# A written engine order for the late stage of an attention-and-feed-forward kernel, and earlier reloads of two chunks' partial outputs

## The chip, the cores and the metric

One core of one Trainium2 chip runs the kernel. The metric is the device time of one execution in microseconds (us), lower is better. The engines that matter are TensorE (PE in the profile; its weight loads are PEld), VectorE (DVE), ScalarE (ACT), GpSimd (POOL) and SyncE (SP), which here only issues DMAs.

## What is computed

```
scores = q @ k^T / 8, masked: heads 0 to 3 see 32 keys back, heads 4 to 7 every 4th of 128
attn   = softmax(scores);  x = (attn @ v), heads side by side: 4608 tokens x 512
h      = x @ w_in                                   # 512 x 2048
g      = max(h, 0) + log1p(exp(-abs(h)))
out    = g @ w_out                                  # 2048 x 512
```

All in float32. A float32 factor goes to TensorE as a high and a low part in the type fp32r (the cast is ACT's, the subtraction DVE's), and three products (high x high, high x low, low x high) make one.

## The kernel before

The 4608 tokens are nine chunks of 512, and the 2048 columns of `w_in` are sixteen tiles of 128 (`ff`). Chunks 0 and 1 are worked while the weights arrive and are decoded: 32 slots of one chunk and one `ff`, in the runs `RUNS`; a slot is twelve 512-column products for h (`h_part`) and, two slots later, twelve for out (`o_part`). Chunk 0 stops after six `ff` and chunk 1 has its first ten; their partial sums go to DRAM (`kept`), and when the runs resume and end, the partial sum is loaded into a buffer `ob` (`ob_tile`) and DVE adds it to what PSUM holds.

Chunks 2 to 8 make the **late stage**, a loop over 56 pairs of `ff` tiles (eight per chunk). A pair makes its h by seven block products instead of eight. Each of the seven steps of `steps` is six 256-column matmuls into one of two PSUM banks (`h_x`, `h_y`), one DVE instruction that brings the bank out (`aside`, to `temps` or `hs`), and then one group of three 512-column matmuls for an output of an earlier tile (`outputs`; two groups in the seventh step). A product overwrites or adds to its bank, so it waits for DVE to have read what the same bank held. After steps 6 and 7 the tile's softplus follows: three activations on ACT, an add on DVE (`e`), the cast `gh` on ACT and the subtraction `gl` on DVE.

Between them stands the attention of the next chunk, in four groups of two heads: scores on PE (`s_ps`), mask and maximum on DVE (`s`, `nm`), eight exponentials on ACT, the sum's reciprocal on DVE (`sm`, `ri`), the division on POOL, a transpose on DVE (`squares`), its way through DRAM by DMA (`turned`, `pt`), and values on PE (`a_ps`), which ACT copies to `x_full`. From `x_full` DVE forms four `sums` (`combine`) and seven blocks are split in high and low (`split`) for the next chunk's products. `convert` brings the weights to the form that the seven products want, six pairs of them during the slots and two in the late stage.

What sets the order: the program's text gives one order, in which `attend`, `combine`, `split` and `convert` are placed by a list of events with due times in slots (`at`, `pump`). The recording layer's scheduler then orders each engine by its own estimate, except instructions that are pinned with `tc.keep_in_program_order`: all matmuls, the DMAs of `load_dma`, and, while `opening` is set (the first seven slots), everything that goes through `pin`. So in the late stage DVE and ACT stand as the scheduler put them.

```
def pin(ins):
    if opening:
        tc.keep_in_program_order(ins)
```

The last output group of a chunk frees its PSUM bank by a copy to `ob` (ACT or DVE, L865 and L867) and goes out from there.

Of the kernel before, what the change touches and what calls it, by code (L numbers as in the profile page):

```python
# [90 lines left out]
def tile_windowed_attention_softplus_ffn(  # L91
# [32 lines left out]
    opening = True  # L124

    def pin(ins):

        if opening:
            tc.keep_in_program_order(ins)
# [114 lines left out]
    def combine(c, n):  # L244

        if n % 2 == 0:
            combined[c, n // 2] = const.tile([P, 2, 2, HALF], F32, name="sums", tag=f"x_{'cd'[n // 2]}")
        dst = [combined[c, j // 2][:, j % 2] for j in range(n + 1)]
# [6 lines left out]
        nc.vector.tensor_tensor(out=dst[n], in0=a, in1=b, op=op)  # L255
# [4 lines left out]
    def split(c, name):  # L260
        if name not in blocks:
# [3 lines left out]
        dst, n = blocks[name], int(name[1:])  # L265
        if name[0] == "a":
            src = x_block(c, n // 10 - 1, n % 10 - 1)
        else:
            src = combined[c, (n - 1) // 2][:, (n - 1) % 2]
        nc.scalar.copy(out=dst[:, 0], in_=src)  # L270
        nc.vector.tensor_tensor(out=dst[:, 1], in0=src, in1=dst[:, 0].bitcast(F32), op=ALU.subtract)

    class Group:
# [50 lines left out]
        def maximum(self):  # L324
# [15 lines left out]
            for r in range(2):  # L340
# [6 lines left out]
                nc.vector.scalar_tensor_tensor(  # L347
                    out=dst, in0=src, scalar=1.0 / 8.0, in1=m, op0=ALU.mult, op1=ALU.add
                )
            nc.vector.tensor_reduce(out=nm, in_=self.blocks, axis=AX.X, op=ALU.max, negate=True)  # L350
# [53 lines left out]
        def turn_squares(self):  # L404

            squares = const.tile([P, WKEYS // SQ, NB, SQ], F32, name="squares", tag="q1")
            nc.vector.transpose(out=squares, in_=self.blocks.rearrange("p t (b k) -> p b t k", k=SQ))
# [97 lines left out]
    events = []  # L505

    def at(when, part, *what):
        events.append((when, len(events), part, what))
# [12 lines left out]
    def pump(now):  # L521
        while events and events[0][0] <= now:
            _, _, part, what = events.pop(0)
            part(*what)

# [56 lines left out]
    def ob_tile(m, resumed, c):  # L582
        if resumed and c:
            if m % 2 == 0:
                obs["both"] = const.tile([P, 2, CH], F32, name="ob", tag=f"x_{'cd'[m // 2]}")
            obs[m] = obs["both"][:, m % 2]
        else:
            obs[m] = dpool.tile([P, CH], F32, name="ob", tag="a")
        if resumed:
            nc.sync.dma_start(out=obs[m], in_=kept[c, m])  # L590

    def o_part(i, m):
# [6 lines left out]
        if m == 0:  # L599
# [3 lines left out]
            if final:  # L603
# [8 lines left out]
        if final:  # L612
# [11 lines left out]
            if m == 0:  # L624
                ob_tile(3, resumed, c)

# [49 lines left out]
    opening = False  # L676
# [10 lines left out]
    def weight_sum(p, j):  # L687
# [8 lines left out]
        nc.vector.tensor_tensor(  # L696
            out=sums[p, j].rearrange("p k n -> p (k n)"), in0=parts[:, 0], in1=parts[:, 1], op=ALU.add
        )

    def weight_13(p):  # L700
# [3 lines left out]
        nc.vector.tensor_tensor(out=d[:, 0], in0=two[:, 0], in1=one[:, 0], op=ALU.subtract)  # L704
        nc.vector.tensor_tensor(out=d[:, 1], in0=two[:, 1], in1=two[:, 0], op=ALU.subtract)

    def weight_24(p):
        d, one, two = diffs[p], sums[p, 0], sums[p, 1]
        nc.vector.tensor_tensor(out=two[:, 1], in0=two[:, 1], in1=d[:, 0], op=ALU.subtract)
        nc.vector.tensor_tensor(out=one[:, 1], in0=one[:, 1], in1=two[:, 1], op=ALU.subtract)  # L710

    def parted(high, low, src):
        nc.scalar.copy(out=high, in_=src)
        nc.vector.tensor_tensor(out=low, in0=src, in1=high.bitcast(F32), op=ALU.subtract)
# [17 lines left out]
    def convert(p):  # L732
# [5 lines left out]
        weight_split_24(p)  # L738

# [37 lines left out]
    for j in range(NPR):  # L777
        attend(FIRST, j, 10.8 + 3.5 * j, (0.5, 2.8, 3.2, 4.5))
# [4 lines left out]
    for p in range(NPAIR):  # L783
        at(20.5 + 1.9 * p if p < EARLY else 36.5 + 3 * (p - EARLY), convert, p)
    for c in range(FIRST + 1, NCH):
        base = 2 * NFF + (c - 1 - FIRST) * NFF
        for j in range(NPR):
            attend(c, j, base + (3.73 * j - 2.1 if c == FIRST + 1 else 3.5 * j - 1.5), (0.5, 2.25, 2.65, 4.5))
        for n in range(4):
            at(base + 13.7 + 0.1 * n, combine, c, n)  # L790
# [254 lines left out]
```

## Time and profile before

| | |
|---|---|
| three runs | 907.26, 908.34, 908.34 us; median 908.34 |
| the profiled execution | 907.07 us, its span 905.3 us |
| granted TensorE clock, mean | 0.998 |
| late stage, first product of pair 0 to first of pair 55 | 236.50 to 882.25 us |

The profile is of one execution. The span runs from the first to the last instruction; about 1.8 us of the execution's time lie around it. PE's busy time counts a pipelined matmul as longer than the step to the next, so PE at 97% says little; how long a pair takes from first product to first product says more.

### The profile page before, as it was taken

What the parts mean: (1) busy time and instruction counts of PE and PEld (TensorE: products, weight loads), DVE (VectorE), ACT (ScalarE), POOL (GpSimd) and SP (SyncE); (2) the same over time, 40 slices, a digit from 0 to 9 for tenths busy, and PEclk for the clock granted to TensorE, in tenths of its full rate; (3) what the DMA queues carried; (4) which work ended last, traced back from release to release, by engine and by line L of the source; (5) the groups of instructions that cost most, each with busy time, mean ns of one, the idle gap of its engine ahead of it and who ended that gap; (6) DMA issues with size and microseconds to landing.
All of it is one profiled execution on the core that took longest, in us unless ns stands there. A gap on an engine that the chain in (4) does not pass through costs nothing.

```text
span 905.3 us, 18339 instructions
## 1 busy us (share of the span) xinstructions
PE 879.8 (97%) x6972; PEld 742.3 (82%) x6978; DVE 634.9 (70%) x1242; ACT 542.0 (60%) x1348; POOL 64.1 (7%) x46
## 2 busy tenths in 40 slices
PE   6899999999999999999999999999999999999998
PEld 3567888788788888888888888888888888889987
DVE  4799998997696586657666675668665866575444
ACT  6677677775555576556555665556555655564443
POOL 1320000000000000000000001000000000000000
PEclk9999999999999999999999999999999999999999
DMA  9989334333555546554555446545654455424223
GB/s 295 315 277 375 131 135 155 129 104 107 190 171 162 163 141 217 170 162 156 198 183 180 161 159 203 185 147 171 203 166 157 166 200 164 152 94 158 98 94 117
DMA packets 79095, 156.41 MB, mean 173 GB/s; under 512 B 8864, under 2 KB 21792, under 8 KB 79008
## 3 DMA queue, kind: packets, MB, share of 16 engines
q1 hardware_dynamic: 78432, 154.18, 51.2%
q8 instruction: 55, 0.90, 0.4%
q10 hardware_dynamic: 576, 1.07, 0.3%
q14 instruction: 32, 0.26, 0.1%
HBM read 124.28 MB, written 30.93 MB: 171 GB/s over the span
## 4 chain that ended last, share of the span: by engine, by line
PE 79%; DVE 12%; ACT 5%; DMA 2%; issue 2%; ACTq 0%; SPq 0%; DVEq 0%
PE o_ps L189 37%; PE h_x L189 17%; PE h_y L189 12%; PE h_ps L189 7%; PE a_ps L189 3%; ACT s L356 2%; PE s_ps L189 2%; DVE e L552 1%; DVE gl L573 1%; DVE s L347 1%; ACT e L547 1%; DMA k<-kpl 1%; DVE nm L350 1%; DMA out_t<-ob 1%; DVE a L162 1%
## 5 line engine op out<-in xcount | busy, mean ns | idle before, releaser
L189 PE MATMUL o_ps<-gh,t 128*128 128x512 f32 (+1 forms) x904 | 341.6, 391 | 0.0
L189 PEld LDWEIGHTS o_ps<-gh,t 128*128 128x128 f32 x904 | 169.7, 188 | 21.4
L189 PE MATMUL o_ps<-gl,t 128*128 128x512 f32 (+1 forms) x452 | 178.3, 394 | 0.0
L545 ACT ACTIVATE e<-hs 128x512 f32<-128x512 f32 x112 | 69.9, 629 | 162.2 <-DVE hs L833 160.7
L567 ACT CAST gh<-e 128x512 fp32r<-128x512 f32 x134 | 82.6, 617 | 65.7 <-DVE e L552 61.2
L552 DVE SCALAR_TENSOR_TENSOR e<-hs,e 128x512 f32<-128x512 f32 x112 | 76.4, 686 | 49.6 <-ACT e L547 49.5
L356 ACT ACTIVATE s<-s,nm 128x96 f32<-128x96 f32 x224 | 80.8, 362 | 48.9 <-DVE nm L350 48.6
L189 PEld LDWEIGHTS h_y<-s,t 128*128 128x128 f32 x672 | 94.6, 188 | 15.7 <-DVE temps L833 5.7
L374 POOL TENSOR_TENSOR s<-s,ri 128x768 f32<-128x768 f32 x36 | 56.9, 1580 | 699.1 <-ACT a L270 162.7
L189 PEld LDWEIGHTS h_x<-a,parts 128*128 128x128 f32 x672 | 92.5, 189 | 16.0 <-DVE hs L833 3.8
L189 PE MATMUL h_x<-a,parts 128*128 128x256 f32 x672 | 101.4, 287 | 2.6 <-DVE temps L831 1.3
L189 PE MATMUL h_y<-s,t 128*128 128x256 f32 x672 | 98.5, 282 | 3.8 <-DVE temps L833 3.6
L573 DVE TENSOR_TENSOR gl<-e,gh 128x512 fp32r<-128x512 f32 x144 | 97.5, 691 | 4.1 <-ACT gh L567 3.7
L546 ACT ACTIVATE e<-e 128x512 f32<-128x512 f32 x144 | 89.0, 625 | 2.1
L547 ACT ACTIVATE e<-e 128x512 f32<-128x512 f32 x144 | 88.4, 625 | 1.9
L189 PE MATMUL h_ps<-xh,parts 128*128 128x512 f32 x256 | 87.2, 397 | 2.2 <-DVE e L552 1.1
L833 DVE TENSOR_TENSOR hs<-h_x,temps 128x256 f32<-128x256 f32 x112 | 47.2, 421 | 59.9 <-PE h_x L189 59.1
L189 PEld LDWEIGHTS o_ps<-gl,t 128*128 128x128 f32 x452 | 86.1, 190 | 3.3 <-DVE gl L573 0.5
L189 PE MATMUL o_ps<-gh,parts 128*128 128x512 f32 x256 | 87.5, 394 | 0.0
L833 DVE TENSOR_TENSOR temps<-h_y,temps 128x256 f32<-128x256 f32 x112 | 46.8, 418 | 26.7 <-PE h_y L189 25.4
L189 PEld LDWEIGHTS h_ps<-xh,parts 128*128 128x128 f32 x256 | 48.1, 188 | 13.8 <-DVE e L552 1.6
L189 PEld LDWEIGHTS o_ps<-gh,parts 128*128 128x128 f32 x256 | 48.1, 188 | 10.3
(81 smaller groups left out, 1263.0 us busy)
## 6 DMA issues: line engine op xcount, KB each, us to landing
t<-w_out SPq DMA_DIRECT2D x224, 256.0 KB, 3.1
raw<-w SPq DMA_DIRECT2D x32, 512.0 KB, 10.1
v<-vp SPq DMA_DIRECT2D x36, 384.0 KB, 4.2
turned<-squares SPq DMA_DIRECT2D x28, 384.0 KB, 3.8
pt<-turned SPq DMA_DIRECT2D x84, 128.0 KB, 2.7
q<-qp SPq DMA_DIRECT2D x36, 256.0 KB, 3.5
w_out<-parts SPq DMA_DIRECT2D x16, 512.0 KB, 2.8
out_t<-ob SPq DMA_DIRECT2D x32, 256.0 KB, 2.1
```

Source lines behind the costliest of these rows:

```text
L162: pin(nc.vector.scalar_tensor_tensor(out=ai, in0=low, scalar=29, in1=ai, op0=ALU.logical_shift_right, op1=ALU.bitwise_or,))
L189: tc.keep_in_program_order(nc.tensor.matmul(**kw))
L347: nc.vector.scalar_tensor_tensor(out=dst, in0=src, scalar=1.0 / 8.0, in1=m, op0=ALU.mult, op1=ALU.add)
L356: pin(nc.scalar.activation(out=self.blocks[:, t], in_=src, func=AF.Exp, bias=self.nm[:, t : t + 1], scale=1.0 / 8.0 if self.masked else 1. ...
L374: pin(nc.gpsimd.tensor_tensor(out=self.blocks, in0=self.blocks, in1=self.ri.unsqueeze(2).to_broadcast([P, NB, WKEYS]), op=ALU.mult,))
L545: pin(nc.scalar.activation(out=e, in_=tiles[i], func=AF.Abs))
L546: pin(nc.scalar.activation(out=e, in_=e, func=AF.Exp, scale=-1.0))
L547: pin(nc.scalar.activation(out=e, in_=e, func=AF.Ln, bias=1.0))
L552: pin(nc.vector.scalar_tensor_tensor(out=e, in0=tiles.pop(i), scalar=0.0, in1=e, op0=ALU.max, op1=ALU.add))
L567: nc.scalar.copy(out=gh, in_=ready[i])
L573: pin(nc.vector.tensor_tensor(out=gl, in0=e, in1=gh.bitcast(F32), op=ALU.subtract))
L833: nc.vector.tensor_tensor(out=dst, in0=src, in1=temps[:, temp], op=ALU.add)
```

## The change

- The `pin` of the late stage holds: `ordered` is set again after the slots, and every DVE and ACT instruction of the late stage, and its DMAs, go through `pin` or `load_dma`. The scheduler no longer orders that stage.
- Each part gets a step of a pair (`step`): the scores after step 6, mask and maximum after step 7, exponentials after step 1, the reciprocal and the division after step 5, the transpose after step 7, and so on (`attend_late`); a tile's softplus, `gh` and `gl` come in the next pair's steps (`late_softplus`); the splits take eight steps around a chunk's start (`shares`), high and low apart.
- `combine` and the last two weight conversions become `chores`, done one at a time where a running estimate of DVE's backlog (`behind`, with a cost for each part) leaves room; `combine` goes in halves of 256 columns.
- The copies that free a finished chunk's banks wait one or two steps behind their matmuls (`finished`).
- Chunk 0's first two reloads go to the buffers `g_x` and `g_y`, idle then, and not to the pool of three that the decoding uses; chunk 1's four loads come behind the last split of chunk 2 (`resumed_tiles`), and each add three steps behind its matmuls (`resumed_part`).
- Chunk 2's four attention groups start 0.2 slots earlier; chunk 3's first two groups start at 26.7 and 29.7 slots (before: 29.9 and 33.63).

```diff
-    opening = True
+    ordered = True
     def pin(ins):
-        if opening:
+        if ordered:
             tc.keep_in_program_order(ins)
...
+        elif resumed and m < 2:
+            obs[m] = const.tile([P, CH], F32, name="ob", tag=f"g_{'xy'[m]}")
         else:
             obs[m] = dpool.tile([P, CH], F32, name="ob", tag="a")
         if resumed:
-            nc.sync.dma_start(out=obs[m], in_=kept[c, m])
+            pin(nc.sync.dma_start(out=obs[m], in_=kept[c, m]))
...
-        if final:
+        if final and resumed and c:
+            at(now[0] + 3 * STEP, resumed_part, m, c, o_ps[m], cost=0.69)
+        elif final:
...
+    def step(n, k, part, *what, cost=0.0, after=0):
+        at(LATE + 2 * n + STEP * (k + 0.9) + 0.001 * after, part, *what, cost=cost)
+
+    def shares(c):
+        n = (c - FIRST) * NPAIR
+        highs = ((-1, 0), (-1, 3), (-1, 4), (-1, 5), (-1, 6), (0, 0), (0, 1))
+        lows = ((-1, 3), (-1, 4), (-1, 5), (-1, 6), (0, 1), (0, 3), (0, 4))
...
+    def attend_late(n, pair, lag):
+        g = groups[n]
+        step(pair, 5, g.score, after=1)
+        step(pair, 5, load, n + 1, after=2)
+        step(pair, 6, g.maximum, cost=1.98)
+        step(pair + 1, 0, g.exponentials, after=3)
+        step(pair + 1, 4, g.divisor, cost=0.36)
+        step(pair + 1, 4, g.divide)
+        step(pair + 1, 6, turn, n, cost=0.97)
+        step(pair + 2, 0, send, n)
+        step(pair + 2, 3, bring, n)
+        step(pair + 2 + lag // 7, lag % 7, values, n, after=1)
...
+            if c == FIRST + 1 and j < 2:
+                attend(c, j, (26.7, 29.7)[j], (0.5, 2.8, 3.2, (5.0, 4.8)[j]))
+            else:
+                attend_late(c * NPR + j, n - 4 + 2 * j, 11 if j == 0 else 7)
...
     pump(2 * NFF)
-    for name in ORDER[4:]:
-        split(FIRST, name)
+    ordered = True
...
-    def late_softplus(u):
+    def late_softplus(u, n):
         i = len(slots) + u
         tiles[i] = hs.pop(u)
         activated(i)
-        softplus(i)
-        g_high(i)
-        g_low(i)
+        second = u % 2
+        step(n + 1, second, softplus, i, cost=0.69, after=-12)
+        step(n + 1, 3 * second, g_high, i, after=-10)
+        step(n + 1, 5 if second else 2, g_low, i, cost=0.69)
...
-            dst = outs[0][:, m % 2]
-            if m % 2:
-                nc.scalar.copy(out=dst, in_=o_ps[m])
-            else:
-                nc.vector.tensor_copy(out=dst, in_=o_ps[m])
-            nc.sync.dma_start(out=out[m * P : (m + 1) * P, c * CH : (c + 1) * CH], in_=dst)
+            at(now[0] + (1 + (m == 2)) * STEP, finished, m, c, o_ps[m], cost=0.0 if m % 2 else 0.69)
...
+            behind += pump(now[0] + 0.01) + ASIDE - (2.11 if k == 6 else 1.41)
+            while chores and chores[0][:2] <= (n, k) and behind + chores[0][2] < 0.4:
+                _, _, cost, chore = chores.pop(0)
+                chore()
+                behind += cost
+            behind = max(behind, 0.0)
```

Three places show how instructions move. Line numbers are those of each kernel, so they differ between the two; by the old numbers L831 and L833 are `aside`, L552 the softplus add, L573 `gl`, L347 and L350 mask and maximum, L867 a finished bank's copy, L615 a resumed add.

DVE in the second pair of a chunk (the pair in which the finished chunk's banks are copied out), before:

```order
L552 SCALAR_TENSOR_TENSOR e<-hs,e 128x512 x2
L347 SCALAR_TENSOR_TENSOR s<-s_ps,mask 128x384 x2
L573 TENSOR_TENSOR gl<-e,gh 128x512
L831 COPY temps<-h_x 128x256
L573 TENSOR_TENSOR gl<-e,gh 128x512
L867 COPY ob<-o_ps_2989 128x512
L350 TENSOR_REDUCE nm<-s 128x8
L833 TENSOR_TENSOR temps<-h_y,temps 128x256
L831 COPY hs<-h_x 128x256
L833 TENSOR_TENSOR temps<-h_y,temps 128x256
L867 COPY ob<-o_ps_2991 128x512
```

and in the changed kernel:

```order
L362 SCALAR_TENSOR_TENSOR s<-s_ps,mask 128x384 x2
L365 TENSOR_REDUCE nm<-s 128x8
L944 COPY temps<-h_x 128x256
L571 SCALAR_TENSOR_TENSOR e<-hs,e 128x512
L946 TENSOR_TENSOR temps<-h_y,temps 128x256
L571 SCALAR_TENSOR_TENSOR e<-hs,e 128x512
L962 COPY ob<-o_ps_3047 128x512
L944 COPY hs<-h_x 128x256
L592 TENSOR_TENSOR gl<-e,gh 128x512
L946 TENSOR_TENSOR temps<-h_y,temps 128x256
L260 TENSOR_TENSOR sums<-x_full 128x512
L946 TENSOR_TENSOR hs<-h_x,temps 128x256
```

Between the pair's first and second read of a product bank (both write `temps`) three instructions stood, `gl`, the copy `ob` and the maximum; now one softplus add does, the maximum stands ahead of the first read, and the copies have gone behind the second and (out of the piece) the fifth.

DVE where the slots end and pair 0 begins, before (the first `temps` is step 1 of pair 0, and the last row is the add of a resumed partial sum):

```order
L407 STREAM_TRANSPOSE squares<-s 128x768
L271 TENSOR_TENSOR a_2761<-x_full,a_2761 128x512
L573 TENSOR_TENSOR gl<-e,gh 128x512
L831 COPY temps<-h_x 128x256
L552 SCALAR_TENSOR_TENSOR e<-h_ps,e 128x512
L573 TENSOR_TENSOR gl<-e,gh 128x512
L833 TENSOR_TENSOR temps<-h_y,temps 128x256
L831 COPY hs<-h_x 128x256
L833 TENSOR_TENSOR temps<-h_y,temps 128x256
L833 TENSOR_TENSOR hs<-h_x,temps 128x256
L833 TENSOR_TENSOR hs<-h_y,temps 128x256
L615 TENSOR_TENSOR ob<-o_ps_2578,ob 128x512
```

and in the changed kernel:

```order
L422 STREAM_TRANSPOSE squares<-s 128x768
L571 SCALAR_TENSOR_TENSOR e<-h_ps,e 128x512
L592 TENSOR_TENSOR gl<-e,gh 128x512
L571 SCALAR_TENSOR_TENSOR e<-h_ps,e 128x512
L592 TENSOR_TENSOR gl<-e,gh 128x512
L944 COPY temps<-h_x 128x256
L946 TENSOR_TENSOR temps<-h_y,temps 128x256
L284 TENSOR_TENSOR s_2846<-sums,s_2846 128x512
L944 COPY hs<-h_x 128x256
L946 TENSOR_TENSOR temps<-h_y,temps 128x256
L284 TENSOR_TENSOR a_2848<-x_full,a_2848 128x512
L946 TENSOR_TENSOR hs<-h_x,temps 128x256
```

The low parts of the splits (L271, now L284) come between the reads of pair 0; the last slots' two `gl` now both stand ahead of the first read, and the resumed add goes to pair 1.

SP's queue in the seventh slot (`kept` and `ob` are the partial sums, `w_out` a store of weights, `q` and `k` an attention group's inputs), one piece of the difference:

```order
-L621 DMA kept<-ob 128x512 x4
-L761 DMA w_out<-parts 128x1024 x2
+L644 DMA kept<-ob 128x512 x2
+L611 DMA ob<-kept 128x512 x2
+L644 DMA kept<-ob 128x512 x2
+L825 DMA w_out<-parts 128x1024
```

Two reloads of chunk 0 now stand right behind the stores that they read, ahead of two more stores.

## Rows read from the trace of the kernel before

**Rows 1.** The page: busy time of each engine, and the chain's shares by engine.

```profile
PE 879.8 (97%) x6972; PEld 742.3 (82%) x6978; DVE 634.9 (70%) x1242; ACT 542.0 (60%) x1348; POOL 64.1 (7%) x46
...
PE 79%; DVE 12%; ACT 5%; DMA 2%; issue 2%; ACTq 0%; SPq 0%; DVEq 0%
```

**Rows 2.** Timeline of PE: first product of pairs 0, 8, 9, 10, 14, 15, 48, 55 (start, length).

```profile
236.50 0.40 PE L189 MATMUL h_x<-a,parts 128*128 128x256 f32 x2
...
332.60 0.40 PE L189 MATMUL h_x<-a,parts 128*128 128x256 f32 x2
...
344.08 0.39 PE L189 MATMUL h_x<-a,parts 128*128 128x256 f32 x1
...
357.50 0.28 PE L189 MATMUL h_x<-a,parts 128*128 128x256 f32 x1
...
404.36 0.52 PE L189 MATMUL h_x<-a,parts 128*128 128x256 f32 x3
...
416.18 0.40 PE L189 MATMUL h_x<-a,parts 128*128 128x256 f32 x2
...
808.47 0.52 PE L189 MATMUL h_x<-a,parts 128*128 128x256 f32 x3
...
882.25 0.40 PE L189 MATMUL h_x<-a,parts 128*128 128x256 f32 x2
```

**Rows 3.** Waits of PE from 236.5 to 882.2 us (total us, times, longest).

```profile
PE h_y L189 <- DVE temps L833: 3.8, 6, 0.7
```

**Rows 4.** Timeline of pair 9: DVE and the two products that waited.

```profile
347.42 0.98 PE L189 MATMUL h_x<-a,parts 128*128 128x256 f32 x6 [0.25 <-DVE temps L831]
...
347.88 0.68 DVE L867 COPY ob<-o_ps 128x512 f32<-128x512 f32 x1
...
348.48 0.94 DVE L350 TENSOR_REDUCE nm<-s 128x8 f32<-128x768 f32 x1
...
349.81 0.98 PE L189 MATMUL h_y<-s,t 128*128 128x256 f32 x6 [0.72 <-DVE temps L833]
```

**Rows 5.** Timeline of pair 55, without waits: products 4 and 5, and the latter's read.

```profile
886.47 0.87 PE L189 MATMUL h_y<-s,t 128*128 128x256 f32 x6
...
887.88 0.87 PE L189 MATMUL h_x<-s,t 128*128 128x256 f32 x6
...
888.79 0.42 DVE L833 TENSOR_TENSOR hs<-h_x,temps 128x256 f32<-128x256 f32 x1 [0.98 <-PE h_x L189]
```

**Rows 6.** Groups by line, 332.6 to 808.5 us (count; busy us, mean ns; idle before).

```profile
L552 DVE SCALAR_TENSOR_TENSOR e<-hs,e 128x512 f32<-128x512 f32 x80 | 54.5, 686 | 33.5 <-ACT e L547 33.5
L573 DVE TENSOR_TENSOR gl<-e,gh 128x512 fp32r<-128x512 f32 x80 | 53.2, 681 | 0.0
...
L347 DVE SCALAR_TENSOR_TENSOR s<-s_ps,mask 128x384 f32<-128x384 f32 x38 | 19.4, 552 | 11.0 <-PE s_ps L189 11.0
...
L356 ACT ACTIVATE s<-s,nm 128x96 f32<-128x96 f32 x152 | 54.9, 362 | 40.9 <-DVE nm L350 40.6
```

**Rows 7.** Timeline: a division on POOL and DVE around it.

```profile
427.20 0.19 DVE L371 RECIPROCAL ri<-sm 128x8 f32<-128x8 f32 x1
427.31 0.64 DVE L271 TENSOR_TENSOR s<-sums,s 128x512 fp32r<-128x512 f32 x1
...
427.56 1.72 POOL L374 TENSOR_TENSOR s<-s,ri 128x768 f32<-128x768 f32 x1 [32.53 <-ACT a L270]
427.87 1.96 DVE L271 TENSOR_TENSOR a<-x_full,a 128x512 fp32r<-128x512 f32 x1
```

**Rows 8.** Timeline of PE in pair 0: a wait for the last slots' `gl`.

```profile
238.61 0.50 PE L189 MATMUL o_ps<-gl,parts 128*128 128x512 f32 x1 [1.00 <-DVE gl L573]
```

**Rows 9.** Windows: busy us of PE, PEld, DVE, ACT, POOL, clock, DMA share, GB/s.

```profile
100.00:200.00 100.00, 98.86 (x624) 80.02 (x623) 95.76 (x178) 74.78 (x178) 6.56 (x4) 1.00 0.37 131
200.00:236.50 36.50, 36.50 (x216) 29.77 (x215) 28.58 (x56) 24.12 (x56) 1.47 (x1) 1.00 0.39 127
```

**Rows 10.** DMA issues by line: count, KB each, median us from issue to landing.

```profile
kept<-ob SPq DMA_DIRECT2D x8, 256.0 KB, 2.3
```

More of the change, by code (lines that the diff above doesn't have):

```diff
@@ L242, in x_block, with combine @@
         return x_half(c, k)[:, :, i * HALF : (i + 1) * HALF]
[L244 to L248, printed above, removed]
+    def combine(c, n, piece=None):
+        for j in range(2):
+            if (c, j) not in combined:
+                combined[c, j] = const.tile([P, 2, 2, HALF], F32, name="sums", tag=f"x_{'cd'[j]}")
+        dst = [combined[c, j // 2][:, j % 2] for j in range(4)]
         a, b, op = (
@@ L254, in combine @@
         )[n]()
-        nc.vector.tensor_tensor(out=dst[n], in0=a, in1=b, op=op)
+        out = dst[n]
+        if piece is not None:
+            out, a, b = (x[:, piece] for x in (out, a, b))
+        pin(nc.vector.tensor_tensor(out=out, in0=a, in1=b, op=op))
     ORDER = ("a11", "s2", "a12", "s3", "s1", "a22", "s4")
@@ L406, in turn_squares @@
             squares = const.tile([P, WKEYS // SQ, NB, SQ], F32, name="squares", tag="q1")
[L407 removed]
+            pin(nc.vector.transpose(out=squares, in_=self.blocks.rearrange("p t (b k) -> p b t k", k=SQ)))
             self.squares = squares
@@ L503, in values, with at @@
         load_v(n + 1)
-    events = []
-    def at(when, part, *what):
-        events.append((when, len(events), part, what))
+    events, serial = [], itertools.count()
+    def at(when, part, *what, cost=0.0):
+        heapq.heappush(events, (when, next(serial), cost, part, what))
     def send(n):
@@ L521, in pump @@
     def pump(now):
+        spent = 0.0
         while events and events[0][0] <= now:
-            _, _, part, what = events.pop(0)
+            _, _, cost, part, what = heapq.heappop(events)
             part(*what)
+            spent += cost
+        return spent
     STEPS = 2 * NKT
@@ L566, in g_high @@
         else:
-            nc.scalar.copy(out=gh, in_=ready[i])
+            pin(nc.scalar.copy(out=gh, in_=ready[i]))
         ready[i] = ready[i], gh
@@ L602, in o_part @@
                     o_ps[k] = bank(f"o_ps{k}", f"o{k}")
-            if final:
+            if final and not (resumed and c):
                 for k in range(3):
@@ L625, in o_part, with resumed_tiles, resumed_part @@
                 ob_tile(3, resumed, c)
+    STEP = 2 / 7
+    now = [0.0]
+    def resumed_tiles(c):
+        for m in range(NKT):
+            ob_tile(m, True, c)
+    def resumed_part(m, c, src):
+        pin(nc.vector.tensor_tensor(out=obs[m], in0=src, in1=obs[m], op=ALU.add))
+        load_dma(out=out[m * P : (m + 1) * P, c * CH : (c + 1) * CH], in_=obs[m])
     def softplus_tile(i):
@@ L675, in tile_windowed_attention_softplus_ffn @@
     load_v(2 * NPR)
-    opening = False
+    ordered = False
     sums, diffs, homes, rests = {}, {}, {}, {}
@@ L738, in convert, with chores_of, homes_13, homes_2 @@
         weight_split_24(p)
+    def chores_of(p):
+        one = lambda: (homes[p][:, 0], homes[p][:, 1], diffs[p])
+        two = lambda: (*second(p), sums[p, 1][:, 1])
+        three = lambda: (*(wt[2 * p + 1, 0][:, part, :HALF] for part in range(2)), sums[p, 0][:, 1])
+        def homes_13():
+            homes[p] = const.tile([P, 2, 2, HALF], F32R, name="t13", tag=f"w{2 * p}_1")
+            weight_13(p)
+            high_part(*one())
+        def homes_2():
+            if p < NPAIR - 1:
+                rests[p] = const.tile([P, 2, 2, HALF], F32R, name="t2", tag=f"w{2 * p + 1}_1")
+            weight_24(p)
+            high_part(*two())
+            high_part(*three())
+        return [
+            (0.69, lambda: weight_sum(p, 0)), (0.69, lambda: weight_sum(p, 1)), (0.84, homes_13),
+            (0.84, homes_2), (0.69, lambda: low_part(*one())), (0.42, lambda: low_part(*two())),
+            (0.42, lambda: low_part(*three())),
+        ]
     def factors(p, name):
@@ L793, in tile_windowed_attention_softplus_ffn @@
+    for c in range(FIRST, NCH):
+        shares(c)
+    step(0, 4, resumed_tiles, 1, after=9)
     for i in range(OPENED + 1, len(slots)):
@@ L893, in tile_windowed_attention_softplus_ffn @@
     )
+    ASIDE, behind = 0.42, 0.0
     between = {0: (1, 1, 1, 1, 0, 1, 1), 1: (1, 1, 0, 0, 1, 1, 2)}
```

102 lines of the change are left out of this document (68 added, 34 removed).

## The prediction

> **What bounds the kernel.** First the page: PE is busy 97% and has 79% of the chain that ended last, DVE 12% [rows 1]. So PE sets the time, and what it doesn't need is where it waits for DVE. A matmul's busy time overlaps the next one's, so I took PE's timeline for the length of a pair. The last seven quiet pairs, without attention, take (882.25 - 808.47)/7 = 10.54 us each; a step is 887.88 - 886.47 = 1.41 us and the seventh, with two output groups, 10.54 - 6 x 1.41 = 2.08 [rows 2, 5]. Pair 8 holds one scores group and takes 11.48 us, pair 14 one values group and 11.82: 0.94 and 1.28 us for a group [rows 2].
>
> With these prices the late stage has a floor. From 236.50 to 882.25 us are 55 pairs, 645.75 us. The floor is 55 x 10.54 = 579.7, less 12 output matmuls that pairs 0 and 1 don't have (a group of three takes half of a 1.41 us step, so 0.23 each, 2.8), plus 23 scores groups (21.6) and 24 values groups (30.7): 629.2 us. So **16.5 us** are above the floor. Pairs 0 to 7 take 96.10 us against 84.3 - 2.8 + 4 x 0.94 + 4 x 1.28 = 90.4: 5.7 of them. Pairs 8 to 47 have the other 10.8. Pair 9 alone takes 13.42 us with one values group, 1.60 over pair 14 [rows 2], and the pattern repeats in pairs 17, 25, 33 and 41: 8.0 us. The last 2.8 are spread in pieces of 0.1 to 0.4.
>
> Why pair 9 is long: two products wait there, 0.25 and 0.72 us, for DVE's reads of the product banks, and DVE was at the copy of a finished chunk's bank and at a maximum, 0.68 and 0.94 us, in front of the read [rows 4]. All such waits on L833's `temps` are 3.8 us, six times [rows 3]; that view counts only from a matmul's modelled end, so pair lengths show more.
>
> **The change, part by part.** No matmul is added or dropped. One scores and one values group leave the late stage for the slots: same price there, nothing on PE.
>
> *The written order on DVE.* I put down when each read of a product bank can start and when it is needed, in a second pair of a chunk, t = 0 at product 1. A read can start 0.91 us after its product's start and takes 0.42 [rows 5]; product k+2 uses the bank, but product 1 of the next pair the bank of product 7. The earlier pair's read 7 ends at -2.08 + 0.91 + 0.42 = -0.75. Mask (2 x 0.55) and maximum (0.94) run to 1.29; read 1 ends at 1.71, needed at 2.82. Softplus 0.69, read 2 at 2.82 (needed 4.23); softplus, copy 0.68, read 3 at 4.61 (5.64); `gl` 0.68, read 4 at 5.71 (7.05); a sum 0.7, read 5 at 6.97 (8.46); `sm` and `ri` 0.4, copy 0.68, read 6 at 8.47 (11.95). None is late [rows 4, 6, 7]. Then `gl`. POOL's division starts 0.36 after `ri` does and takes 1.72 us, so from 7.5 to 9.3 here. A DVE instruction of two SBUF operands that started 0.31 us into a division took 1.96 us and not 0.64, ending 0.55 after POOL [rows 7]. So this `gl` ends at 9.8, read 7 at 10.25, needed at 10.54: **0.3 us of slack**, the thinnest place. By the Trainium skill (SBUF — State Buffer, Who interferes with whom) a DVE instruction with two SBUF inputs contends with a GpSimd instruction that reads SBUF, and the pair of ports is an exclusive lock; the trace agrees with its 1.96 us. That rule speaks against standing `gl` behind the division in every odd pair.
>
> So the five long pairs give back 8.0 us. Of the scattered 2.8 I take half, 1.4 (ends 0 and 2.8), since a restart of PE after a short wait may stay.
>
> *Splits.* In a chunk's last pair two low parts more (2 x 0.68) stand between reads 5 and 7: read 7 ends at 11.6, against 10.54, or 11.82 where the pair has a values group, as five of the six do. Bounds 0 and 1.1 us each; I take 0.2 x 5 = 1.0 lost, near the lower end since the values group stands ahead of step 6.
>
> *Pairs 0 to 7.* In pair 0 PE waits 1.0 us for the last slots' `gl` [rows 8], which stood behind a transpose and a low part; now nothing but the softplus is between. The four resumed adds now stand one in a step of pair 1. DVE's queue in pair 1 is then 7 reads (2.9), two softplus, two `gl`, four adds (8 x 0.69), and 0.4 + 0.94 of attention and a sum (0.7): 10.5 us, against 10.54 - 1.4 + 1.28 = 10.4 for a pair with six output matmuls fewer and a values group: full, and a tenth over. Of 5.7 us I take 4.5 (ends 2.5 and 5.7).
>
> *ACT.* It is in written order too, and a cast that waits holds all behind it. In an odd pair `gh` must wait for a softplus that ends at 2.4, is cast by 3.0, and eight exponentials of 0.36 [rows 6] end at 5.9; `sm` wants them at 7.0. Cost nothing; the cover is 1.1 us.
>
> *SP.* Two reloads now stand behind the stores they read, so the queue stops for about 2.3 us [rows 10], once; behind it are two stores of partial sums, one of weights and the inputs of a later group. A store held back keeps a decode buffer 2.3 us longer. Nothing to 2.3 us; I take nothing. For chunk 0's end the reloads in idle buffers free the pool earlier, no gain on PE that I can see.
>
> *The slots.* Chunk 3's second group brings DVE 1.1 + 0.94 + 0.4 + a transpose (taken as the maximum's 0.94, of the same 128x768): 3.4 us before 236.5, where DVE is idle 36.5 - 28.6 = 7.9 us of the last 36.5 [rows 9]. It hides there; without that cover, 3.4 us. From 100 to 200 us DVE is busy 95.8 of 100 us [rows 9], and a scheduler that sees other work will order it otherwise: -2 to +3 us, taken as 0.
>
> **Sum:** 8.0 + 1.4 - 1.0 + 4.5 = 12.9 us. The sum is made on the profiled execution's 907.07 us: 894.2. It lies 0.2 below the fastest and 1.3 below the median of the runs shown, and I put the forecast at 894.5.
>
> **Rivals.**
> - *The bubbles are the two banks'.* The Trainium skill (Perfetto Trace Analysis, Optimization Strategy) says of a gap that repeats in a stretch that it can mean too little SBUF or PSUM for the next tile. Products have two banks; if a bank and not the order is short, another queue order moves the wait to another step. For it: the waits of pair 9 are for reads of these banks. Against: the quiet pairs run on the same two banks without a wait, and the reads in pair 9 came late behind named work [rows 4]. Then the 9.4 us stay and 3.5 come: 903.6.
> - *The slots pay.* Re-ordered decoding at 95.8% DVE, and the held buffer: 3 to 5 us back, 897 to 899.
> - *Slower: `ri` late.* The thin place fails. If the exponentials end over 1.1 us later than I put them, `ri`, the division and the locked `gl` move with them, and beyond the 0.3 us of slack all of it is PE's, in each of 22 odd pairs. From `ri` 0.97 us late on, (12.9 + 1.8)/22 = 0.67 us a pair eat the gain and more; at 1.3 late it is 894.2 + 22 = 916. For it: a written order can't let a read pass. Against: 1.1 us of cover on ACT.
> - *No change:* DVE's waits come back one for one at other steps (splits at their bound of 5.3, pairs 0 to 7 at their lower end, half the bubbles): about 906.5 to 908.
>
> **How the numbers follow.** Forecast 0.65 (890.5, all 16.5 us, to 899 with every lesser end), the slots 0.12, the banks 0.10, slower 0.08, no change 0.05. A difference under 0.2% (1.8 us) can't be told from none here. Faster: 0.65 + 0.12 + 0.10 = 0.87; same 0.05; slower 0.08. The range 890 to 904 takes in the forecast, the slots and the banks' case, and leaves out the last two.
>
> **What would show it.** Right: pairs 9, 17, 25, 33 and 41 at about 11.8 us, and waits of PE for `temps` and `hs` near none after 262 us; 236.5 us for the first product of pair 0, within 2. Splits right: the last pair of a chunk within 0.3 of its floor. Wrong: the same waits at step 1 in odd pairs (locked `gl`), ACT's exponentials or casts as the releaser of DVE, PE waits between 100 and 236 us, or long pairs at the old places.

## The result and the profile after

| | before | after |
|---|---|---|
| median of the runs | 907.80 us (906.33 to 908.34) | 896.43 us (894.22 to 896.88) |
| ratio, with its 95% interval | | 0.9872 [0.9851, 0.9893] |
| the profiled execution, its span | 907.07, 905.3 us | 894.22, 892.4 us |
| granted TensorE clock, mean | 0.998 | 0.997 |
| first product of pair 0 to first of pair 55 | 645.75 us | 630.97 us |

The change is faster by 1.3%. The page of the changed kernel, the lines that answer to [rows 1]:

```profile
PE 874.4 (98%) x6978; PEld 743.4 (83%) x6978; DVE 644.0 (72%) x1257; ACT 554.4 (62%) x1348; POOL 64.7 (7%) x46
...
PE 79%; DVE 13%; ACT 4%; DMA 2%; issue 1%; ACTq 0%; SPq 0%; DVEq 0%
```

Shares hardly move, as PE bounds both. The pair lengths tell more. PE's timeline after, the first product of pairs 0, 8, 9, 10, 48 and 55 (start, length), against [rows 2]:

```profile
237.73 0.97 PE L190 MATMUL h_x<-a,parts 128*128 128x256 f32 x6
...
331.04 0.88 PE L190 MATMUL h_x<-a,parts 128*128 128x256 f32 x6
...
342.60 0.88 PE L190 MATMUL h_x<-a,parts 128*128 128x256 f32 x6
...
354.38 0.88 PE L190 MATMUL h_x<-a,parts 128*128 128x256 f32 x6
...
794.92 0.88 PE L190 MATMUL h_x<-a,parts 128*128 128x256 f32 x6
...
868.70 0.88 PE L190 MATMUL h_x<-a,parts 128*128 128x256 f32 x6
```

Pair 9 takes 354.38 - 342.60 = 11.78 us where it took 13.42, and pairs 17, 25, 33 and 41 take 11.79. The last seven quiet pairs take 10.54 as before. Waits of PE from 236 to 880 us, all of them, where before had 7.7 us in 16, the largest group of them in [rows 3]:

```profile
PE h_x L190 <- DVE temps L944: 1.1, 1, 1.1
PE o_ps L190 <- DVE gl L592: 0.2, 1, 0.2
```

One wait for a read is left, in pair 0. Why the others went is read from DVE's own waits for ACT, 236 to 880 us. Before:

```profile
DVE e L552 <- ACT e L547: 46.4, 56, 2.1
...
DVE sm L368 <- ACT s L356: 20.9, 22, 1.6
```

and after, all that there is of DVE's waits for ACT but 0.4 us:

```profile
DVE gl L592 <- ACT gh L586: 2.5, 2, 1.8
DVE s L284 <- ACT s L280: 1.1, 1, 1.1
DVE e L571 <- ACT e L566: 0.7, 1, 0.7
```

Before, DVE stood 67.3 us in front of a softplus add or the exponentials' sum, with whatever read came next in its queue behind it. In pair 9 it stood 1.71 us in front of the two adds ahead of read 1, DVE before:

```profile
343.62 0.69 DVE L552 SCALAR_TENSOR_TENSOR e<-hs,e 128x512 f32<-128x512 f32 x1 [1.22 <-ACT e L547]
344.80 0.69 DVE L552 SCALAR_TENSOR_TENSOR e<-hs,e 128x512 f32<-128x512 f32 x1 [0.49 <-ACT e L547]
...
346.94 0.42 DVE L831 COPY temps<-h_x 128x256 f32<-128x256 f32 x1
```

In the written order each comes late enough for ACT to be done. No run takes these waits away by themselves, so what share of the gain is theirs is argued from the trace, not shown. The groups from 331 to 795 us after, against [rows 6], say the same of `e` (idle before it 33.5 us then, 0.0 now), and show what the written order costs on `gl`, 822 ns where it was 681:

```profile
L592 DVE TENSOR_TENSOR gl<-e,gh 128x512 fp32r<-128x512 f32 x80 | 65.8, 822 | 0.0
L571 DVE SCALAR_TENSOR_TENSOR e<-hs,e 128x512 f32<-128x512 f32 x80 | 54.5, 682 | 0.0
```

**Where the 12.9 us of span went, by stages.** In pairs 8 to 47, by the prediction's prices, 10.8 us above the floor became 1.0 (331.04 to 794.92 is 463.9 us; 40 x 10.54 + 18 x 0.94 + 19 x 1.28 = 462.8): 9.8 gained. Pairs 0 to 7 take 93.3 us for 96.1: 2.8 gained. One scores and one values group less in the stretch: 2.2. Together the 14.8 us of the table. The moved groups come back in the slots: from the 33rd h matmul of the slots to pair 0 it is 184.3 us for 182.5, 1.8 more, put down to these groups by their prices. The start up to that matmul was 0.6 shorter, and what follows pair 55's first product 0.7 longer (23.7 for 23.0). 14.8 - 1.8 + 0.6 - 0.7 = 12.9.

The other runs of the changed kernel are about 2 us above the profiled one. The start can explain that much: over twelve profiles of it and its variants the 33rd h matmul begins at 53.4 to 55.7 us, and the profiled run has the 53.4. Those with 53.4 to 53.9 have a mean granted clock of 0.997 or 0.998, those with 54.4 and more 0.989 to 0.996; the three other runs, which left no trace, have 0.993 to 0.996. The kernel before has 54.0, and b_pinall below, its variant, 53.4; whether the change itself makes the start longer is not settled by them.

### The profile page after: what moved, and what is told of

Same layout as the page of the kernel before. It is cut to its first block, busy times and chain, and to the rows that moved or that the text cites. A ratio compares the mean times of both kernels' runs of the same rounds, so it can differ in the third digit from the quotient of the medians.

```text
span 892.4 us, 18303 instructions
## 1 busy us (share of the span) xinstructions
PE 874.4 (98%) x6978; PEld 743.4 (83%) x6978; DVE 644.0 (72%) x1257; ACT 554.4 (62%) x1348; POOL 64.7 (7%) x46
## 3 DMA queue, kind: packets, MB, share of 16 engines
q10 hardware_dynamic: 576, 1.07, 0.4%
## 4 chain that ended last, share of the span: by engine, by line
PE 79%; DVE 13%; ACT 4%; DMA 2%; issue 1%; ACTq 0%; SPq 0%; DVEq 0%
PE o_ps L190 38%; PE h_x L190 18%; PE h_y L190 14%; PE a_ps L190 4%; PE s_ps L190 2%; ACT s L371 2%; PE h_ps L190 2%; DVE a L168 1%; DVE e L571 1%; DVE a L163 1%; DVE gl L592 1%; DVE a L154 1%; DVE b L730 1%; DVE a L158 1%; DMA kept<-ob 1%
## 5 line engine op out<-in xcount | busy, mean ns | idle before, releaser
L592 DVE TENSOR_TENSOR gl<-e,gh 128x512 fp32r<-128x512 f32 x144 | 113.0, 785 | 3.7 <-ACT gh L586 3.2
L190 PEld LDWEIGHTS h_x<-a,parts 128*128 128x128 f32 x672 | 94.4, 189 | 12.5 <-DVE temps L944 1.6
L190 PE MATMUL h_x<-a,parts 128*128 128x256 f32 x672 | 98.4, 282 | 1.1 <-DVE temps L944 1.1
L565 ACT ACTIVATE e<-e 128x512 f32<-128x512 f32 x144 | 91.1, 633 | 4.2
L566 ACT ACTIVATE e<-e 128x512 f32<-128x512 f32 x144 | 91.1, 632 | 4.2
```

The costliest lines, as they stand in the source:

```text
L190: tc.keep_in_program_order(nc.tensor.matmul(**kw))
L565: pin(nc.scalar.activation(out=e, in_=e, func=AF.Exp, scale=-1.0))
L566: pin(nc.scalar.activation(out=e, in_=e, func=AF.Ln, bias=1.0))
L592: pin(nc.vector.tensor_tensor(out=gl, in0=e, in1=gh.bitcast(F32), op=ALU.subtract))
```

## Experiments

The read-out that the start can't disturb is "the stretch", first product of pair 0 to first product of pair 55: 631.0 us in the changed kernel, 645.7 before (which has one scores and one values group more in it, 2.2 us). Two profiles of the changed kernel have 630.97 and 630.91. b_pinall, e_gl2, e_gl3, e_div5, e_reload, e_stack and e_old9 were executed once each. The times of one kernel spread by up to 5 us (894.22 to 899.53 in the nine runs of the changed one), so it is the stretches and pairs that are compared, and some tenths of a us in a single pair can be chance.

### Is it the fixed order, or the new places in the text?

The changed kernel without the pin in the late stage:

```diff
     pump(2 * NFF)
-    ordered = True
```

> The changed kernel with the late stage's DVE and ACT left to the scheduler again (the program's text, with its new places, stays). Theory (the fixed order on DVE is what ends the long pairs): the scheduler stacks copy, reduction and gl ahead of reads again, part of the 12.9 us goes back, 899 to 905 us, and PE waits for temps in the second pairs of the chunks. Rival (the new places in the text are enough, the scheduler keeps close to them): within 1 us of the changed kernel, 895 to 897.

Measured: 916.12 us, ratio to before 1.008 [1.0065, 1.0095], stretch 650.2. Slower than both kernels and outside what either theory gave: the direction was right, the size not. The largest group of PE's waits from 236 to 880 us, and pair 7's end on DVE and PE:

```profile
PE h_x L190 <- DVE hs L945: 10.4, 17, 1.2
```

```profile
332.50 1.98 DVE L284 TENSOR_TENSOR a<-x_full,a 128x512 fp32r<-128x512 f32 x1
...
336.21 0.97 DVE L422 STREAM_TRANSPOSE squares<-s 128x768 f32<-128x768 f32 x1
337.11 0.38 DVE L945 TENSOR_TENSOR hs<-h_y,temps 128x256 f32<-128x256 f32 x1
337.42 0.67 DVE L284 TENSOR_TENSOR a<-x_full,a 128x512 fp32r<-128x512 f32 x1
338.01 0.41 DVE L945 TENSOR_TENSOR hs<-h_x,temps 128x256 f32<-128x256 f32 x1
...
338.57 0.71 PE L190 MATMUL h_x<-a,parts 128*128 128x256 f32 x4 [1.24 <-DVE hs L945]
```

Five instructions (one of them locked behind POOL, 1.98 us) stand between reads 5 and 6, and a split's low part between 6 and 7: product 1 of pair 8 waits 1.24 us. All odd pairs from 5 to 43 are 0.5 to 1.5 us over their floor. The matmuls and the text are those of the changed kernel, so this is the order of what the pin holds, on DVE, ACT and POOL, alone: 19 us of the stretch. DVE's waits for ACT in front of the adds and the sum are 38.8 us here, less than before, and the stretch is longer all the same: what stands ahead of the reads counts too.

The other half, the kernel before with its late stage held in the order of its text, every DVE, ACT and DMA instruction in this way:

```diff
+    opening = True
...
-            nc.vector.tensor_copy(out=dst, in_=src)
+            pin(nc.vector.tensor_copy(out=dst, in_=src))
```

> The kernel before, its text as it was, with every DVE and ACT instruction of the late stage (and its DMAs) held in the order of the text: the pin without the new places. Theory (an order of the text is only as good as the places in it): each softplus add, cast and gl now stands right behind the read that feeds it, so DVE waits for three activations and a cast (some 4.1 us) behind reads 6 and 7 of every pair; product 1 is about 2.4 us late and product 3 about 1.7: 56 x 4.1 = 230 us more, 1050 to 1150 us. Rival (holding the order is what gains, wherever it is): below 905 us.

Measured: 1262.97 us. Quiet pairs take 14.68, 4.14 over 10.54, the 4.1 that was worked out; pairs with attention are up to 12 over. DVE's waits from 236 to 1240 us:

```profile
DVE e L552 <- ACT e L547: 222.6, 110, 2.0
DVE gl L573 <- ACT gh L567: 81.5, 111, 1.0
DVE sm L368 <- ACT s L356: 71.3, 23, 3.1
```

Over the floor of the prediction's prices the stretch has 371 us, of which 4.14 a pair are 228. Of the other 143 the expectation lacked at least two things. One is the third row: in that text `sm` too stands where DVE must wait for the exponentials, 3.1 us in each of 23 groups. The other is the clock: behind such waits PE was granted the lower of its two levels again and again, 0.89 on average from 331 to 1100 us. How much each costs is not shown. So neither half gains by itself: places without the pin lose 0.8%, the pin without places 39%.

### Which places counted

A finished chunk's bank copies right behind their matmuls:

```diff
-            at(now[0] + (1 + (m == 2)) * STEP, finished, m, c, o_ps[m], cost=0.0 if m % 2 else 0.69)
+            finished(m, c, o_ps[m])
```

> The changed kernel with a finished chunk's four bank copies right behind their output matmuls, not one or two steps later. Theory (pairs 9, 17, 25, 33, 41 were long because copy, maximum and two gl stood together ahead of one read; a copy alone is covered, reads 2 to 5 of these pairs have 1.3 to 1.5 us of slack in the changed kernel's trace and a copy takes 0.69): within 0.7 us of the changed kernel, about 896. Rival (it is the copies' later place that ended the long pairs): 1.6 us for each of five pairs comes back, about 904.

Measured: 899.45 us, ratio 0.989 [0.9868, 0.9911], stretch 634.9, 3.9 more where 0.7 at most was expected. Pairs 9, 17 and 25 are at 11.81 to 11.82, so the theory held for the reads; but pairs 33 and 49 were 1.8 and 1.6 us long, for a reason that it lacked. Pair 33 on ACT and DVE:

```profile
636.63 0.58 ACT L960 COPY ob<-o_ps 128x512 f32<-128x512 f32 x1 [4.00 <-DMA out_t<-ob]
637.12 0.62 ACT L586 CAST gh<-e 128x512 fp32r<-128x512 f32 x1
...
637.77 0.69 DVE L592 TENSOR_TENSOR gl<-e,gh 128x512 fp32r<-128x512 f32 x1 [2.96 <-ACT gh L586]
```

There are two buffers `ob` for four copies, so the fourth waits until the second's store has landed, 4.0 us here; the cast behind it on ACT waits along, then `gl` on DVE, then read 7. The delay in `finished` gives that store more time, but it is not shown to cover it: in the changed kernel the fourth copy still waits 1.7 to 2.6 us for it in five of six chunks, at no cost to PE, and in e_stack below, which keeps the delay for this copy, it waits 3.95 us in pair 33. For the reads the delay isn't needed.

Mask and maximum behind read 1, with the first copy at once:

```diff
-        step(pair, 6, g.maximum, cost=1.98)
+        step(pair + 1, 0, g.maximum, cost=1.98, after=-20)
...
+            at(now[0] + (m > 0) * (1 + (m == 2)) * STEP, finished, m, c, o_ps[m], cost=0.0 if m % 2 else 0.69)
```

> The changed kernel with maximum and mask put between reads 1 and 2 of every odd pair with an attention group, and a finished chunk's first bank copy right behind its matmuls, ahead of read 2 too. The prediction named these two, in front of a read, as what made pair 9 long. Theory now (read 2 has about 3 us of room there, these take 1.05 + 0.9 + 0.6, and the pile of before had two softplus adds and two gl as well): the stretch from pair 0 to pair 55 within 1 us of 631. Rival (the two suffice): 1 us or more for each of pairs 9, 17, 25, 33 and 41, 636 to 639.

And the whole old order in front of five pairs:

```diff
+        if old9(n):        # n = 8, 16, 24, 32, 40
+            step(n, 6, softplus, i, cost=0.69, after=5)
+            step(n, 6, g_high, i, after=6)
+            step(n + (second > 0), 0 if second else 6, g_low, i, cost=0.69, after=-30 if second else 7)
+            return
```

(the mask and the maximum are placed as in the run before, but in these five pairs alone; the copies as there, in all chunks).

> The changed kernel with the whole old order in front of pairs 9, 17, 25, 33 and 41 alone, still fixed: both softplus adds and a gl ahead of read 1, then the second gl, mask, maximum and the bank copy ahead of read 2. Theory (the pile as a whole is the cause): read 2 ends about 0.9 us late, and with the restart each of these five pairs takes 1.0 to 1.6 us more; the stretch is 636 to 639, the other pairs as in the changed kernel. Rival (DVE's order isn't what made these pairs long): within 1 us of 631.

Measured: stretch 645.9 (910.49 us) and 649.6 (914.90 us). Both theories fell short, on one mechanism. In e_stack pairs 9, 17, 25 and 41 are 0.4 us over, but so are nearly all odd pairs (0.8 in the last of a chunk), and pair 33 has 2.5, with the store's wait again. In e_old9 the five pairs are 2.5 to 5.4 us long. Pair 9 of e_old9:

```profile
348.57 1.02 DVE L362 SCALAR_TENSOR_TENSOR s<-s_ps,mask 128x384 f32<-128x384 f32 x2
...
349.22 0.98 PE L190 MATMUL a_ps<-pt,v 96*64 96x64 f32 x26 [2.49 <-issue]
```

The values group `a_ps` takes its bank from the same tag as the scores (`att`, in `score` and `values`), so it starts when the first mask (0.55 us of the two) has read the scores: 348.57 + 0.55 = 349.12, and PE at 349.22. The profile names no releaser for this wait ("issue"); the banks' tag and the times say it. With mask and maximum behind read 1 the values group of the same pair is late, and everything on PE behind it. The five such waits of e_old9 are 12.4 us of its 18.7. The rest lies in pairs 9, 33 and 41, 4.1 to 5.4 us long: behind the wait PE was granted 0.50, the lower of its two levels, for some us (351.50 to 353.50 in pair 9). Pairs 17 and 25, with the same wait at a granted clock of 1.00, are 2.6 long. So these two runs show that the mask's place ahead of read 1 matters, by 0.4 to 2.5 us a pair, for PE's attention bank. They don't price the old pile by itself. That the copy and the maximum alone made pair 9 long was argued in the prediction and isn't borne out: e_stack puts them there, and in pair 9 nothing waits for read 2.

### The thin place: `gl` behind the division

First the chain itself, pair 9 of the changed kernel, DVE and POOL:

```profile
350.93 0.20 DVE L386 RECIPROCAL ri<-sm 128x8 f32<-128x8 f32 x1
...
351.30 1.47 POOL L389 TENSOR_TENSOR s<-s,ri 128x768 f32<-128x768 f32 x1 [22.81 <-DVE ri L386]
...
351.79 0.42 DVE L946 TENSOR_TENSOR hs<-h_y,temps 128x256 f32<-128x256 f32 x1
352.13 1.19 DVE L592 TENSOR_TENSOR gl<-e,gh 128x512 fp32r<-128x512 f32 x1
353.25 0.41 DVE L946 TENSOR_TENSOR hs<-h_x,temps 128x256 f32<-128x256 f32 x1
```

`gl` takes 1.19 us and ends 0.55 after POOL, as in [rows 7]. Read 7 ends at 353.66, and product 1 of pair 10 starts at 354.38: 0.72 us to spare, 0.3 forecast. From the same rows of every odd pair: 0.06 in pair 1, 0.13 in pairs 17, 25, 33 and 41, 0.48 to 0.54 in eleven, 0.63 in the last pair of a chunk. The 0.13 comes of one copy: in pair 17 the second bank copy stands ahead of `sm` (444.15 us), in pair 9 behind `ri`, so the division and `gl` end 0.6 us later there. Two kernels lengthen the chain, by doing the second tile's `gl` over again in odd pairs, once and twice:

```diff
+        if second and n % 2 == 0:
+            for _ in range(1):
+                step(n + 1, 5, g_again, i)
```

> The changed kernel with the second tile's gl done twice over in every odd pair, right behind the division (0.61 us more on DVE ahead of read 7, nothing else). Read-out: first product of pair 0 to first of pair 55, 631.0 us in the changed kernel. Theory (read 7 has the slack that the changed kernel's trace shows, 0.48 to 0.54 us in 11 odd pairs, 0.13 in pairs 17, 25, 33, 41, 0.63 to 0.76 in the others, and PE pays only what is beyond): 4.6 us more, 635.6. The prediction's own figure (0.3 us of slack in each of 22): 6.8 more, 637.8. Rival (read 7 isn't what product 1 of the next pair waits for): no more than 0.5.

> The same with gl done three times (1.22 us more ahead of read 7 in every odd pair). Theory by the slacks of the changed kernel's trace: 20.6 us more, 651.6 for the same stretch. The prediction's figure (0.3 us of slack in 22 pairs): 20.2 more. Rival (some other wait takes it up, since DVE is busy only 72%): under 10 more.

Measured: stretches 640.7 (+9.7; 904.77 us) and 658.8 (+27.8; 922.16 us). PE's waits, with one and with two repeats:

```profile
PE h_x L190 <- DVE hs L952: 2.7, 5, 0.7
```

```profile
PE h_x L190 <- DVE hs L952: 20.7, 23, 1.4
```

Read 7 is what product 1 of the next pair waits for, and beyond the slack PE pays: the second repeat costs 18.1 us, 0.73 in nearly every odd pair with a division. Both sums were too low, by 5 and 7 us, for two reasons. A repeat put read 7 not 0.61 but 0.73 us later (in pair 11 it ends 11.98 us behind product 1, for 11.25). And a late pair lost more than its lateness: pair 11, 0.19 us late by that, takes 12.03 us for 11.79, and pair 12 11.66 for 11.56, so stopping and starting cost some 0.15 us there. With 0.7 us more of DVE work ahead of read 7 in every odd pair the changed kernel loses most of its gain, and with 1.5 it is slower than before.

The lock itself, with `ri` and the division one step later:

```diff
-        step(pair + 1, 4, g.divisor, cost=0.36)
-        step(pair + 1, 4, g.divide)
+        step(pair + 1, 5, g.divisor, cost=0.36)
+        step(pair + 1, 5, g.divide)
```

> The changed kernel with ri and the division one step later, behind read 6 and right ahead of the second tile's gl. Theory (a DVE instruction of two SBUF operands waits only when it starts after the division has begun; the division starts some 0.25 us behind ri, so gl starts first): gl's mean falls from 785 to about 690 ns, the division isn't shorter, and the stretch from pair 0 to pair 55 stays within 0.5 us of 631.0, since the lock was covered. Rival (the lock takes either of the two, so POOL or gl is just as late, and the transpose that follows, now later, pushes read 1 of the next pair): 3 us or more slower.

Measured: stretch 636.1 (901.38 us). In all odd pairs from 3 on but the last ones of the chunks read 7 has 0.76 us to spare and nothing is lost. The 5.2 us are in pairs 7, 15, 23, 31 and 39, 1.07 each, where a split's low part also stands there. Pair 15:

```profile
425.81 0.64 DVE L284 TENSOR_TENSOR a<-x_full,a 128x512 fp32r<-128x512 f32 x1
...
426.06 1.72 POOL L389 TENSOR_TENSOR s<-s,ri 128x768 f32<-128x768 f32 x1 [21.66 <-DVE ri L386]
...
426.36 1.96 DVE L592 TENSOR_TENSOR gl<-e,gh 128x512 fp32r<-128x512 f32 x1
```

The low part starts 0.25 us ahead of the division and takes its 0.64, and POOL 1.72 for 1.47; `gl` starts 0.3 behind it and takes 1.96. "Issue order, not op shape, decides who blocks", says the Trainium skill (SBUF — State Buffer, Who interferes with whom), and the trace agrees: of two like instructions the one that is first is free and the other pays 1.3 us. The theory overlooked the second instruction in these five pairs, and the rival's size (3 us or more) came from them alone.

### The reload in idle buffers

```diff
-        elif resumed and m < 2:
-            obs[m] = const.tile([P, CH], F32, name="ob", tag=f"g_{'xy'[m]}")
```

> The changed kernel with chunk 0's first two reloads in the decoding's pool again, as in the kernel before. Read-out: from the 65th matmul of the slots' h to the first product of pair 0, which leaves the start, where the weights' first DMAs decide, out: 182.5 us in the profile of before, 184.3 in that of the change. Theory (the slots are longer by the scores and values group that was moved into them, and the reload's place costs and gains nothing): 184.3 within 0.5. Rival (the reloads that stop SP's queue are what costs): about 182.5.

(The stretches in that text count from the 33rd h matmul; from the 65th both are 20.8 shorter.) Measured: 187.3 us, 3.0 more, where no difference was expected: the theory fell, and its rival (182.5) too. Near 220 us PE waits twice, 1.7 us together, for DVE's resumed adds, and these for their loads:

```profile
216.75 0.69 DVE L636 TENSOR_TENSOR ob<-o_ps,ob 128x512 f32<-128x512 f32 x1 [1.03 <-DMA ob<-kept]
...
218.57 0.69 DVE L636 TENSOR_TENSOR ob<-o_ps,ob 128x512 f32<-128x512 f32 x1 [0.26 <-DMA ob<-kept]
...
220.44 0.69 DVE L636 TENSOR_TENSOR ob<-o_ps,ob 128x512 f32<-128x512 f32 x1 [1.18 <-DMA ob<-kept]
```

All four loads take their buffer from the decoding's pool of three here, and land too late for their add. Behind the second wait PE was granted 0.50, the lower of its two levels (221.80 to 225.00 us), and its products step by 0.43 us there, not 0.23: part of the 3.0 us is the clock's. But the stretch is 628.9, 2.1 us shorter: while PE waited and ran slowly, DVE and ACT caught up, and pair 0 has no wait at all. By these two profiles the reload's new place is worth 0.9 us net (896.71 us in one run, within the changed kernel's spread).

### Two repairs of pair 0 and pair 1

Pair 0 is still 12.27 us long. Its front on ACT, DVE and PE:

```profile
240.80 0.62 ACT L586 CAST gh<-e 128x512 fp32r<-128x512 f32 x1
...
241.45 0.69 DVE L592 TENSOR_TENSOR gl<-e,gh 128x512 fp32r<-128x512 f32 x1 [1.79 <-ACT gh L586]
242.06 0.42 DVE L944 COPY temps<-h_x 128x256 f32<-128x256 f32 x1
...
242.53 0.74 PE L190 MATMUL h_x<-a,parts 128*128 128x256 f32 x4 [1.15 <-DVE temps L944]
```

Read 1 stands behind the last slot's `gl`, whose cast ACT does after three split casts. The slots are still the scheduler's, and the pinned late stage inherits what it left. Moved behind read 2:

```diff
+        if i < len(slots) - 1:
+            g_low(i)
+        else:
+            step(0, 1, g_low, i, cost=0.69, after=-12)
```

> The changed kernel with the last slot's gl behind read 2 of pair 0, and not ahead of read 1. Theory (pair 0 is still 1.7 to 2.1 us over its floor because read 1 stands behind this gl, which waits for a cast that ACT does after three split casts): read 1 starts some 2.3 us earlier, product 3 doesn't wait, pair 0 gives 1.0 to 1.4 us, 895.2 us where the changed kernel has a median of 896.4. Rival (the wait moves to the output matmuls that read this gl, or to read 2): no gain, within 0.3 us of the changed kernel.

Measured: 893.92 us (893.40 to 896.38), ratio 0.9842 [0.9824, 0.986]; read 1 starts 1.70 us behind the first product, not 4.33; pair 0 takes 10.71 us and the stretch 629.5, 1.5 less. That is a little more than expected. Of the 2.5 us between the medians the stretch accounts for 1.5. DVE after it:

```profile
240.06 0.41 DVE L947 COPY temps<-h_x 128x256 f32<-128x256 f32 x1
241.22 0.42 DVE L949 TENSOR_TENSOR temps<-h_y,temps 128x256 f32<-128x256 f32 x1 [0.74 <-PE h_y L190]
241.93 0.69 DVE L592 TENSOR_TENSOR gl<-e,gh 128x512 fp32r<-128x512 f32 x1 [0.29 <-ACT gh L586]
```

With this and the resumed adds earlier (`at(now[0] + (2, 2, 1, 2)[m] * STEP, resumed_part, ...)`), beside the changed kernel on one chip:

> The changed kernel with two repairs: the last slot's gl behind read 2 of pair 0 (as tried before), and chunk 1's resumed adds one step earlier (the third two steps), so that they don't stand in the two steps of pair 1 that have no output matmuls. Theory (pair 0 and pair 1 are what is left above the floor): pair 0 gives 1.5 us and pair 1 0.3 to 0.4, the stretch from pair 0 to pair 55 is 629.1 and the median 1.8 us under that of the changed kernel beside it. Rival (the adds earlier wait for their reload and hold DVE): pair 1 longer than 10.9 us, no better than the first repair alone (629.5).

> The changed kernel once more, on the same chip as the three beside it, to compare them with. 894 to 897 us; from the first product of pair 0 to the first of pair 55 again 631 us, whatever the start costs.

Measured: changed kernel 896.77 us, ratio 0.9881 [0.9859, 0.9903], stretch 630.9; both repairs 895.50, ratio 0.9862 [0.9846, 0.9878], stretch 630.4. The second repair did harm: pair 1 takes 11.45 us for 10.86, by the rival. The third add stands in front of read 3 and waits for its load:

```profile
256.36 0.69 DVE L658 TENSOR_TENSOR ob<-o_ps,ob 128x512 f32<-128x512 f32 x1 [0.38 <-DMA ob<-kept]
256.97 0.41 DVE L947 COPY hs<-h_x 128x256 f32<-128x256 f32 x1
```

So the first repair alone has the lowest median: 1.5 us less than the change on the stretch, and ahead of the kernel before by 1.6%.

## Why the prediction was right, point by point

- **The time.** Forecast 894.5, measured 896.43, inside 890 to 904. On the profiled execution the sum gave 894.2, which is what it took, but that near a hit is luck, by terms that cancel: the late stage gained 12.6 of its own (12.9 forecast), the slots 0.4 and the start 0.6, the end lost 0.7.
- **Long pairs, 8.0.** Right: all five came down to 11.8. The sign of it that was named, waits for `temps` and `hs` near none after 262 us, is there. The reason was too narrow, and half of it misread: of pair 9's two waits only that for read 2 stood behind the copy and the maximum, while read 1 stood behind two adds, the mask and a `gl`, after 1.71 us of DVE's waiting for ACT. The copy and the maximum by themselves don't do it (e_stack). That an order which puts reads behind other work does, e_free shows; DVE standing for ACT, 67.3 us in all before, is the other part, argued from the trace.
- **Scattered, 1.4 of 2.8, and splits, 1.0 lost.** Both too dark. Pairs 8 to 47 gained 9.8 where 8.0 + 1.4 - 1.0 = 8.4 were forecast; the chunks' last pairs take 11.81 us, on the floor. Nothing of the split's bound of 1.1 us came, for the reason that the prediction gave, the values group ahead of step 6: in pair 15 DVE waits 1.27 us for PE behind it, and read 7 ends 11.2 us behind product 1 (11.6 worked out), 0.6 before it is needed.
- **Pairs 0 to 7, 4.5.** The step that was mis-sized: 2.8, near the lower end of 2.5. What it says of DVE's queue, "now nothing but the softplus is between", left out ACT, where three split casts had come ahead of the cast that this `gl` needs; e_gl31 shows 1.5 us for it. Pair 1 was rightly called full: reads 3 and 4 end 0.09 and 0.05 us before their products there, and it is 0.4 over.
- **The locked `gl`.** Right as a mechanism, and the slack of 0.3 lies among the measured 0.06 to 0.72. But the pair worked out has no values group, which every odd pair with a division has here (11.8 us long, not 10.54): both the reads and what needs them came about 1 us later, so that the slack came near is partly luck. The rival built on it didn't come, since the exponentials end 2.0 us ahead of `sm` in pair 9 (cover of 1.1 forecast), but its price is real: 1.5 us more in front of read 7 gave 922.16 us.
- **The banks' rival** fell: the same two banks, no bubbles. By the Trainium skill (Perfetto Trace Analysis, Optimization Strategy) such a gap can mean too little memory for the next tile; here it didn't.
- **Slots and SP, 0.** The slots pay 1.8 us for 2.2 of moved groups, as forecast ("same price there"). That the reload has no gain on PE was wrong: without it the slots are 3.0 us longer, 0.9 net (e_reload).
- **A sum of the range.** "Every lesser end" of the terms gives 8.0 + 0 - 5.3 + 2.5 = 5.2 us and 901.9 us, not 899. It lies under 904 too, and the forecast doesn't hang on it.

## What to carry to other kernels

An engine's queue is in order, so a wait in it is paid by everything behind it (in e_copies a cast on ACT came behind a copy's 4.0 us): list for each engine the instruction that PE needs soonest and what may stand in front of it, and put an instruction that needs another engine's result as late as its reader allows. Holding an order was worth nothing here without such places (b_pinall), and the places nothing where the scheduler could undo them (e_free). Before moving one, look for what else it frees (an attention bank, an `ob` buffer behind a store), since that wait has no name in the old profile.

## What the runs showed that was not expected

- A wait of PE costs some 0.15 us beyond its length, most of it in the pair behind (e_gl2).
- One late store of 256 KB came through three engines: 4.0 us on ACT, 2.96 on DVE, 1.8 on PE (e_copies).
- A pause of PE can be nearly free: 3.0 us lost in the slots, to two waits and the clock behind them, gave 2.1 back in pair 0, where DVE and ACT were what was late (e_reload).
- A wait can cost more than its length through the clock: behind 2.5 us of standing PE was granted 0.50 in three pairs of five, and these are 1.5 to 2.9 us longer than the other two (e_old9).
- In b_pinall (the fixed old order), where PE waits up to 7.8 us at a time, the mean granted clock was 0.912, a mix of the two levels of 1.2 and 2.4 GHz, against 0.998 before; the page's row of it, in 40 slices, falls behind the eighth slice (the late stage starts in it):

```profile
PEclk9999999987898888888998889988898888998999
```
